# A two-block transformer kernel: block sums of the second chunk placed behind residual additions, and the third layer's deviations computed in a step of their own

## The chip, the core and the metric

One NeuronCore of a Trainium2 chip. The metric is device time in microseconds for one launch, median of several runs; lower is better. The engines are TensorE (PE in the profile, its weight loads PEld), VectorE (DVE), ScalarE (ACT), GpSimd (POOL) and SyncE (SP), which here only issues DMAs. Each works through its own queue of instructions and they meet at semaphores.

## The reference

Four layers in a row on one sequence of 2048 tokens by 1024 features, each added to the residual x:

```python
x = x + _A_ref(_layernorm(x), A_wqkv, A_wo)              # layer 0
x = x + _B_ref(_layernorm(x), B_W_gate, B_W_up, B_W_down)  # layer 1
x = x + _A_ref(_layernorm(x), A_wqkv, A_wo)              # layer 2
x = x + _B_ref(_layernorm(x), B_W_gate, B_W_up, B_W_down)  # layer 3

# _A_ref: linear attention, 32 heads of 32
q, k, v = x @ wqkv;  phi(t) = where(t > 0, t + 1, exp(t)) + 1e-6
o = phi(q) @ (phi(k).T @ v) / (phi(q) . sum(phi(k)) + 1e-6);  result = o @ wo
# _B_ref: gated unit, F = 3584
result = (relu(x @ W_gate) * (x @ W_up)) @ W_down
```

The layer norm subtracts the mean and divides by sqrt(variance + 1e-5), without weights. Inputs and the output are bf16.

## The kernel before

**Tiles.** x stays on chip in fp32 as 16 token tiles of 128 tokens (P = 128, ST = 16). Four tiles make a quarter (QT = 4), two quarters a chunk of 1024 tokens. Layers 1 and 3 (`layer_B`) work on chunk c = 0 and then on c = 1. For each chunk `glu` runs 14 units of gate and up products, and `down` then multiplies the result h by W_down and adds to x.

**Block products.** Most large products are done with seven block products in place of eight (Strassen's scheme in Winograd's form). With four blocks a11, a12, a21, a22 of an operand it needs the sums s1 = a21 + a22, s2 = s1 - a11, s3 = a11 - a21 and s4 = a12 - s2. For the normed and transposed tokens xnT these block sums are made by `sums_x` (L1104, the additions at L1114 to L1117) on VectorE, one call for a pair of token tiles j (one of each quarter of the chunk), four instructions of 128x512 each. `glu` reads them through xs[l, c]; its first product of a later chunk (five, `vg`) reads s1 of all four j.

**The down projection.** `down` runs seven products in the order 11, 21, T1, T2, 22, T3, T4. The large ones (`product`, matmuls at L1253) take 112 or 56 matmuls of 512 columns; each of four PSUM banks is added to x on VectorE when it is done (`onto`, L1266). In layer 3, whose sum is the output, the last addition of a piece goes to a bf16 tile xo (L1273) and is sent to the output. Some products are deep (`deep`, matmuls at L1305): split once more into seven of 14 matmuls of 256 columns. In chunk 0, T1 and 22 are deep in layer 1, and T1, 22 and T4 in layer 3. Within a deep product the order is x = 1, z = 5, y = y + 6, x = x + 2, y = y + 7, z = z + 3, y = y + 4. Before 7 can go onto y, VectorE must have made z from y and m5 (`dz`, L1322; m5 is ScalarE's copy `dm`, L1312). The inner sums of a deep product's operand (h at L1280) are made on VectorE too, shortly before.

**Norms and transposes.** While `down` of chunk 0 runs, the tokens of chunk 1 (quarters 2 and 3) are normed for the same layer by `ln_chunk`. ScalarE makes the normed tile xnb (`ln_norm_sums`, L215 to L221), and `ln_turn` (L400) issues a DMA transpose of it into xnT on SyncE. Eight transposes follow each other, alternating between quarter 2 and quarter 3: the first and second belong to j = 0, the seventh and eighth to j = 3. In layers 0 and 2 `ln_norm` takes statistics on VectorE (L163, L168), and `ln_rstd` takes the reciprocal deviation on ScalarE as exp(-0.5 ln(var + eps)).

**Order.** Work beside the products is put off by `_Later`: `at(delay, fn)` runs fn after so many ticks, and `tick` is called after each product step. `down` of chunk 0 in layer 1 has 54 ticks: 8 for each large product, 7 for each deep one. Ticks 31 and 38 end T2 and 22. So in program order `ln_chunk(l, 1, 20, 3, 3, after)` puts the four calls of `sums_x` at ticks 31, 37, 43 and 49. Outside the `manual_schedule` blocks the framework's planner sets the order of each engine's queue by its own estimate of when operands are ready; an instruction may come out ahead of one written before it. `issue_after(it)` keeps what is written inside it behind the instruction it; `behind` (L265) wraps that.

**Buffers.** Weights, xnT, the sums s and h come from one pool of 16 buffers of 8 KB for each partition (`slot`). A new tile takes a buffer that was released earlier, so the place in the program at which a tile is first asked for decides which buffer it gets and when that is free. Weights come through a ring (`_Ring`) of five tiles ahead, loaded by SyncE.

The names that matter below: `dy`, `dx`, `dz` are the banks of `down` (with T in the name, those of a deep product T1 or T4 in the profile); `w<-td`, `w<-dd`, `w<-ddT` are loads of W_down blocks; `w<-tg`, `w<-tu` loads of the made gate and up blocks; `away<-x` stores of x.

Of the kernel before, what the change touches and what calls it, by code (L numbers as in the profile page):

```python
# [8 lines left out]
ALU = mybir.AluOpType  # L9
ACT = mybir.ActivationFunctionType  # L10
F32 = mybir.dt.float32
# [3 lines left out]
P = 128  # L15
# [2 lines left out]
QT = 4  # L18


LN_AT = ((4, 2), (8, 2), (12, 2), (16, 2), (20, 12), (23, 10), (26, 8), (29, 6))


class _Ring:
# [68 lines left out]
class _Net:  # L93
# [69 lines left out]
        self.nc.vector.bn_stats(out=stats[:, c, :], in_=src[:, c * fmax:(c + 1) * fmax])  # L163

    def ln_rstd(self, stats):
        nc = self.nc
        mv = self.small.tile([P, nc.vector.BN_AGGR_DIM], F32, tag="mv")
        nc.vector.bn_aggr(out=mv, in_=stats)  # L168
        rstd = self.small.tile([P, 1], F32, tag="rstd")
        nc.scalar.activation(out=rstd, in_=mv[:, 1:2], func=ACT.Ln, bias=self.eps5[:, 0:1])  # L170
        self.last_rstd = nc.scalar.activation(out=rstd, in_=rstd, func=ACT.Exp, scale=-0.5)
        return mv, rstd

    def ln_scale(self, src, mv, rstd, xn, h=None):
        w = self.D // 2
# [5 lines left out]
    def ln_norm(self, layer, t):  # L181

        nc = self.nc
        if layer % 2:
            return self.ln_norm_sums(layer, t)
        src = self.xb[t] if layer == 0 else self.x[t]
        stats = self.small.tile([P, 2, nc.vector.BN_STATS_DIM], F32, tag="stats")
        for c in range(2):
            self.ln_stat(t, src, c, stats)
        mv, rstd = self.ln_rstd(stats)  # L190

        def scale():
            if layer % 2 == 0 and (layer, t // QT) != (2, 0):
                return self.ln_scale(src, mv, rstd, self.xn_home(layer, t))
            xn = self.temp([P, self.D], F16, name="xnb") if layer % 2 else self.xn_home(layer, t)
            shift = self.small.tile([P, 1], F32, tag="shift")
            nc.vector.tensor_scalar(out=shift, in0=mv[:, 0:1], scalar1=rstd[:, 0:1], scalar2=-1.0,
                                    op0=ALU.mult, op1=ALU.mult)
            nc.scalar.activation(out=xn, in_=src, func=ACT.Identity, scale=rstd[:, 0:1],
                                 bias=shift[:, 0:1])  # L200
            return xn

        return scale
# [198 lines left out]
    def ln_at(self, delay, layer, t, lag, after=None):  # L402
        def stat():
            with self.tc.issue_after(after) if after else nullcontext():
                scale = self.ln_norm(layer, t)
            self.later.at(1, lambda: norm(scale))

        def norm(scale):
            xn = scale()
            self.later.at(lag, lambda: self.ln_turn(layer, t, xn))  # L410

        self.later.at(delay, stat)

# [40 lines left out]
    def layer_A(self, l, last_ln):  # L454
        nc, G, KT, D = self.nc, self.G, self.KT, self.D
        ring, later = self.ring, self.later
# [32 lines left out]
        def k_unit(q, j, c, between=None):  # L489
            t = q * QT + j  # L490
            pk = self.pk_home(l, t)
            self.phi(project(f"k{c}", q, j, between), pk[:, c * NW:(c + 1) * NW])
            later.at(1 + (10 if self.phi_lag else 0), lambda: k_sum(t, slice(c * NW, (c + 1) * NW)))
# [31 lines left out]
        xn, pk = (lambda i: self.xn[l, i]), (lambda i: self.pk[l, i])  # L525
# [315 lines left out]
        def column_major(f, q):  # L841
            return [lambda j=j, c=c: f(q, j, c) for c in range(H) for j in range(QT)]
# [28 lines left out]
        for i in range(QT if l == 0 else self.NS, self.ST):  # L871
            at, lag = (8 + 3 * (i - QT), 2) if l == 0 else LN_AT[i - self.NS]
            self.ln_at(at, l, i, lag)
            if l:
                later.at(at + 2, lambda i=i: self.send_away(i))
        if l == 0:
            first = self.head_units(lambda *a: k_unit(0, *a), lambda *a: q_unit(0, *a), *steps)
        else:
            first = column_major(k_unit, 0)
# [239 lines left out]
    def ln_chunk(self, l, c, first, step, lag, after):  # L1119
        for j in range(QT):  # L1120
            for h in range(2):
                self.ln_at(first + (2 * j + h) * step, l, (2 * c + h) * QT + j, lag, after)
            self.later.at(first + (2 * j + 1) * step + lag + 5, lambda j=j: self.sums_x(l, c, j))

    def glu(self, l, c, u, hT):

# [81 lines left out]
    def down(self, l, c, hT, final):  # L1208


        nc, later, ring, v = self.nc, self.later, self.ring, self.nc.vector
# [30 lines left out]
        first, second = c * 2 * QT, (c * 2 + 1) * QT  # L1242
# [17 lines left out]
        def onto(ts, cols, src, last):  # L1260

            xs = self.xall[:, ts, cols]
            if len(src.shape) == 2:
                src = src.rearrange("p (t n) -> p t n", n=cols.stop - cols.start)
            if not (final and last):
                v.tensor_tensor(out=xs, in0=xs, in1=src, op=ALU.add)  # L1266
                return
            xo = self.temp([P] + list(xs.shape[1:]), BF16, name="xo")
            m = xs.shape[1]
            split = ts.stop == self.ST and cols.start == 0 and m == 2  # L1270
            for k, queue in zip(range(m) if split else (0,), (nc.scalar if split else nc.gpsimd, nc.sync)):
                s = slice(k, k + 1) if split else slice(0, m)
                v.tensor_tensor(out=xo[:, s, :], in0=xs[:, s, :], in1=src[:, s, :], op=ALU.add)  # L1273
                queue.dma_start(out=self.o_v[:, ts.start + s.start:ts.start + s.stop, cols], in_=xo[:, s, :])

        def sums(ops):
# [150 lines left out]
    def layer_B(self, l, final):  # L1427
        ring = self.ring

        def behind(it, fn):  # L1430
            with self.tc.issue_after(it.ins):
                fn()

        for c in range(2):
            hT = []
            first = l == 1 and c == 0
            wd = {}
            for u in range(self.U):
                if u % 2 == 0:
                    hT.append(self.slot(f"h{l}_{c}_{u // 2}", dtype=F16))  # L1440
                ring.load_to(ring.index((l, c, "g", u)) + 5)
                if first:
                    if u + 1 < self.U:
                        self.later.at(4 if u else 9, lambda u=u: behind(self.last_put if u else self.last_z, lambda: [
                            self.make_gu(ring.get((l, c, w, u + 1)), w, u + 1) for w in "gu"]))
                    if u == 3:
                        for d in (self.U - 4, self.U - 2):
                            wd[d] = self.load_d(d)
                        self.make_dd("22", 18)
                    if u in (4, 5, 6):  # L1450
                        for i, n in enumerate(range(3 * (u - 4), min(3 * (u - 3), 8))):
                            self.later.at(2 + 4 * i, lambda d=self.U - 4 + n // 4 * 2, n=n % 4: behind(
                                self.last_put, lambda: self.sums_d(wd[d], d, (n,))))
                    if u == 7:
                        self.make_dd("T1", 1)
                if not final and c == 1:
                    if u in (0, 3):
                        self.load_w("qk"[u // 3])
                    if u in (1, 2, 4, 5):
                        for n in range(2):  # L1460
                            self.later.at(4 + 5 * n, lambda w="qk"[u // 4], n=2 * (u % 3 - 1) + n: behind(
                                self.last_put, lambda: self.sums_w(w, n)))
                if (l, c, u) in ((1, 1, 6), (3, 0, 4)):
                    self.make_dd("T4" if l == 1 else "21", 1)
                if c == 0 and u == 1:
                    for n, turn in enumerate(self.turns):
                        self.later.at(1 + n, turn)
                if c == 0 and u in (1, 2):
                    self.later.at(6, lambda u=u: behind(self.last_put, self.pairs[u - 1]))
                self.glu(l, c, u, hT)  # L1470
                if c == 0 and u == 2:
                    self.pairs[2]()
                if c == 0 and u == (self.U - 1 if first else 0):
                    after = self.last_put.ins
                if c == 1 and u == 6:
                    held = self.last_put.ins
            if c == 0:
                self.ln_chunk(l, 1, 20, 3, 3, after)
            elif not final:
                self.ln_later(l + 1, 0, 25, 3, 4, held)  # L1480
                self.ln_later(l + 1, 1, 37, 3, 4, held)
            self.down(l, c, hT, final)

    def run(self):
# [56 lines left out]
```

## Time and profile before

| | us |
|---|---|
| median of 3 runs | 1451.38 (1451.16 to 1452.89) |
| the profiled execution, own time | 1451.29 |
| its span | 1449.5 |
| VectorE busy | 959.4 |
| ScalarE busy | 613.8 |
| GpSimd busy | 310.0 |

The profiled execution's own time lies 1.8 us above its span: what runs before the first and after the last recorded instruction. TensorE ran at its full clock in all slices. Down of layer 1, chunk 0 lies at 397 to 479 us of the span, and that of layer 3, chunk 0 at 1117 to 1197 us. In the table of the page's part 2 the DMA engines are busy for four to nine tenths of most slices:

```profile
DMA  9950787997469999646973119978644799444465
```

Each digit is a fortieth of the span (36 us) in tenths. Slices 12 and 13 (counted from 1) hold layer 1's stretch, 32 and 33 that of layer 3.

### The profile page before, as it was taken

How to read it: one execution, taken by the hardware profiler on the slowest of the kernel's cores; microseconds unless marked ns; L12 is line 12 of the kernel's file. 1: busy time of each engine (PE TensorE's matmuls, PEld its weight loads, DVE VectorE, ACT ScalarE, POOL GpSimd, SP SyncE). 2: the span in 40 equal slices, each digit the busy share in tenths (PEclk: the TensorE clock that was granted, in tenths of full speed). 3: DMA queues.
4: the chain of work that ended last, by engine and by line, in shares of the span. 5: the costliest groups of instructions: out<-in, count | busy, mean ns of one | idle time of the engine just before them, and what ended most of it. 6: DMA issues, size and time to landing. Idle time of an engine off the chain costs nothing.

```text
span 1449.5 us, 20266 instructions
## 1 busy us (share of the span) xinstructions
PE 1437.6 (99%) x7430; PEld 709.0 (49%) x7430; DVE 959.4 (66%) x1799; ACT 613.8 (42%) x1113; POOL 310.0 (21%) x221
## 2 busy tenths in 40 slices
PE   9999999999999999999999999999999999999998
PEld 4444444444455444445644444444444564444457
DVE  7978698677594456549688876764445864444595
ACT  7872564233333334332168626633333433333300
POOL 1453861011100011110031586410111011111102
PEclk9999999999999999999999999999999999999999
DMA  9950787997469999646973119978644799444465
GB/s 284 238 161 8 175 215 200 289 331 256 161 217 288 353 312 307 199 128 222 294 244 88 59 32 278 266 230 262 206 145 150 207 279 328 146 145 146 153 236 179
DMA packets 328836, 304.90 MB, mean 210 GB/s; under 512 B 107456, under 2 KB 291776, under 8 KB 327712
## 3 DMA queue, kind: packets, MB, share of 16 engines
q1 hardware_dynamic: 320688, 282.30, 65.5%
q10 hardware_dynamic: 6560, 17.24, 3.2%
q0 software_dynamic: 1488, 4.07, 0.8%
q8 instruction: 58, 0.95, 0.3%
q14 instruction: 42, 0.34, 0.1%
HBM read 227.28 MB, written 51.64 MB: 192 GB/s over the span
## 4 chain that ended last, share of the span: by engine, by line
PE 92%; DVE 4%; ACT 2%; DMA 1%; issue 1%; SPq 0%; ACTq 0%; DVEq 0%
PE yg L1140 10%; PE yu L1140 10%; PE ps L480 10%; PE dy L1253 7%; PE xu L1140 6%; PE xg L1140 6%; PE dx L1253 6%; PE ps L763 4%; PE vg L1140 3%; PE zu L1140 3%; PE vu L1140 3%; PE zg L1140 3%; PE my L562 3%; PE dyT L1305 2%; PE mx L562 2%; PE mv L562 2%
## 5 line engine op out<-in xcount | busy, mean ns | idle before, releaser
L1140 PEld LDWEIGHTS <-w 128*128 128x128 f16 (+1 forms) x3136 | 306.8, 98 | 372.2 <-issue 3.4
L1193 POOL TENSOR_TENSOR h<-m5u,m5g 128x512 f16<-128x512 f32 x56 | 72.6, 1297 | 721.1 <-DVE m5u L1189 648.8
L480 PE MATMUL ps<-w,xnT 128*128 128x512 bf16 x768 | 169.9, 379 | 0.6 <-DMA w<-in_A_wqkv_dram 0.4
L1176 DVE TENSOR_TENSOR zg<-yg,m5g 128x512 f32<-128x512 f32 x56 | 39.1, 698 | 179.5 <-PE yg L1140 175.4
L480 PEld LDWEIGHTS <-xnT 128*128 128x128 bf16 x768 | 74.3, 98 | 90.2 <-issue 1.4
L1140 PE MATMUL yg<-s,w 128*128 128x512 f16 x448 | 115.0, 379 | 0.3 <-DVE zg L1176 0.3
L1140 PE MATMUL yu<-s,w 128*128 128x512 f16 x448 | 114.9, 379 | 0.1
L1140 PE MATMUL xg<-xnT,w 128*128 128x512 f16 x448 | 115.0, 379 | 0.0
L1140 PE MATMUL xu<-xnT,w 128*128 128x512 f16 x448 | 115.0, 379 | 0.0
L1253 PEld LDWEIGHTS <-h 128*128 128x128 f16 x672 | 65.7, 98 | 78.2
L1305 PEld LDWEIGHTS <-h 128*128 128x128 f16 x966 | 94.5, 98 | 15.3 <-issue 3.0
L1148 ACT ACTIVATE m5g<-m5g 128x512 f32<-128x512 f32 x56 | 35.2, 628 | 154.2 <-DVE m5g L1189 154.2
L423 ACT ACTIVATE e<-e,eps 128x512 f32<-128x512 f32 x128 | 91.0, 720 | 3.3
L710 POOL TENSOR_TENSOR kvc<-pq,kvc 128x1024 f32<-128x1024 bf16 x32 | 78.6, 2455 | 53.1 <-DVE den L715 32.7
L1253 PE MATMUL dx<-w,h 128*128 128x512 bf16 x392 | 85.3, 379 | 0.0
L763 PE MATMUL ps<-T,pqT 128*128 128x512 bf16 x384 | 83.6, 379 | 0.0
L1157 ACT ACTIVATE m5g<-vg 128x512 f32<-128x512 f32 x56 | 33.4, 597 | 108.5 <-PE vg L1140 108.5
L1151 DVE TENSOR_TENSOR h<-yu,r 128x512 f16<-128x512 f32 x56 | 38.7, 691 | 52.8 <-PE yu L1140 52.8
L501 POOL TENSOR_TENSOR kvc<-kvc,slab 128x512 f32<-128x512 f32 x46 | 57.3, 1250 | 75.9 <-DVE slab L426 72.7
L1148 ACT ACTIVATE r<-yg 128x512 f32<-128x512 f32 x56 | 33.4, 597 | 85.5 <-PE yg L1140 85.5
L1189 DVE TENSOR_TENSOR m5u<-yu,m5u 128x512 f32<-128x512 f32 x56 | 38.6, 690 | 46.7 <-PE yu L1140 46.7
L422 ACT ACTIVATE e<-ps 128x512 f32<-128x512 f32 x92 | 54.2, 589 | 28.2 <-PE ps L480 27.7
(233 smaller groups left out, 2384.1 us busy)
## 6 DMA issues: line engine op xcount, KB each, us to landing
w<-in_B_W_gate_dram SPq DMA_DIRECT2D x56, 512.0 KB, 6.1
w<-in_B_W_up_dram SPq DMA_DIRECT2D x56, 512.0 KB, 5.9
w<-tg SPq DMA_DIRECT2D x42, 512.0 KB, 7.3
w<-tu SPq DMA_DIRECT2D x42, 512.0 KB, 6.7
w<-ddT SPq DMA_DIRECT2D x21, 896.0 KB, 6.1
w<-td SPq DMA_DIRECT2D x18, 896.0 KB, 4.8
w<-dd SPq DMA_DIRECT2D x15, 896.0 KB, 4.6
w<-in_B_W_down_dram SPq DMA_DIRECT2D x14, 896.0 KB, 4.9
```

Of the source, the lines that this page charges most:

```text
L422: nc.scalar.activation(out=e, in_=ps, func=ACT.Relu, scale=-1.0)
L423: nc.scalar.activation(out=e, in_=e, func=ACT.Exp, scale=-1.0, bias=self.eps6[:, 0:1])
L480: nc.tensor.matmul(by_row(ps), lhsT=self.xnT[l, l_q][:, kt, j * P:(j + 1) * P], rhs=w[:, kt, :].rearrange("p (b i d) -> p i b d", i=R, d=H ...
L501: nc.gpsimd.tensor_tensor(out=ksum[:, cols], in0=ksum[:, cols], in1=pk, op=ALU.add)
L562: nc.tensor.matmul(banks[j], lhsT=A(i)[:, j * P:(j + 1) * P], rhs=B(i), start=start and i == 0, stop=i == NS - 1, skip_group_check=True)
L710: nc.gpsimd.tensor_tensor(out=prod, in0=pq_of[sc, j], in1=zrow, op=ALU.mult)
L763: nc.tensor.matmul(ps, lhsT=pqT[sc][:, g, j * P:(j + 1) * P], rhs=T[g // 4][:, g % 4, n2 * NW:(n2 + 1) * NW], start=(g == 0), stop=(g == G ...
L1140: nc.tensor.matmul(ps, lhsT=W[w][m][:, k, :], rhs=A[m][:, k, :], start=start and k == 0, stop=k == 3, skip_group_check=True)
L1148: self.last_relu = nc.scalar.activation(out=out, in_=ps, func=ACT.Relu)
L1193: nc.gpsimd.tensor_tensor(out=h[:, 3, :], in0=V["u"], in1=V["g"], op=ALU.mult)
L1253: nc.tensor.matmul(banks[j], lhsT=A(k)[:, j * P:(j + 1) * P], rhs=w[:, i, :], start=start and k == 0, stop=k == self.U - 1, skip_group_che ...
L1305: nc.tensor.matmul(bank[:, j * H:(j + 1) * H], lhsT=A[i // 2][:, i % 2, j * P:(j + 1) * P], rhs=B[m][:, i, :], start=start and i == 0 and ...
```

## The change

Two things are changed. `ln_chunk` no longer asks for a call of `sums_x` five ticks after the transpose is issued. It asks for the four calls at ticks 39, 42, 45 and 48, and each is kept behind the last residual addition that `onto` had written by then (`last_on`). And for layer 2 the reciprocal deviation leaves the step that takes the statistics: `ln_norm` stops after `bn_aggr`, the next tick runs `ln_root` (the Ln and Exp pair on ScalarE), and the tick after that scales. The statistics start one tick earlier (LN_AT and the two calls of `ln_later`), and `send_away` keeps its tick.

```diff
--- before.py
+++ after.py
@@ -18,7 +18,7 @@
 QT = 4
 
 
-LN_AT = ((4, 2), (8, 2), (12, 2), (16, 2), (20, 12), (23, 10), (26, 8), (29, 6))
+LN_AT = ((3, 2), (7, 2), (11, 2), (15, 2), (19, 12), (22, 10), (25, 8), (28, 6))
 
 
 class _Ring:
@@ -163,13 +163,16 @@
         self.nc.vector.bn_stats(out=stats[:, c, :], in_=src[:, c * fmax:(c + 1) * fmax])
 
     def ln_rstd(self, stats):
+        mv = self.small.tile([P, self.nc.vector.BN_AGGR_DIM], F32, tag="mv")
+        self.nc.vector.bn_aggr(out=mv, in_=stats)
+        return mv, self.ln_root(mv)
+
+    def ln_root(self, mv):
         nc = self.nc
-        mv = self.small.tile([P, nc.vector.BN_AGGR_DIM], F32, tag="mv")
-        nc.vector.bn_aggr(out=mv, in_=stats)
         rstd = self.small.tile([P, 1], F32, tag="rstd")
         nc.scalar.activation(out=rstd, in_=mv[:, 1:2], func=ACT.Ln, bias=self.eps5[:, 0:1])
         self.last_rstd = nc.scalar.activation(out=rstd, in_=rstd, func=ACT.Exp, scale=-0.5)
-        return mv, rstd
+        return rstd
 
     def ln_scale(self, src, mv, rstd, xn, h=None):
         w = self.D // 2
@@ -187,9 +190,16 @@
         stats = self.small.tile([P, 2, nc.vector.BN_STATS_DIM], F32, tag="stats")
         for c in range(2):
             self.ln_stat(t, src, c, stats)
-        mv, rstd = self.ln_rstd(stats)
-
-        def scale():
+        if layer == 2:
+            mv = self.small.tile([P, nc.vector.BN_AGGR_DIM], F32, tag="mv")
+            nc.vector.bn_aggr(out=mv, in_=stats)
+        else:
+            mv, rstd = self.ln_rstd(stats)
+
+        def scale(rstd=None if layer == 2 else rstd):
+            if rstd is None:
+                rstd = self.ln_root(mv)
+                return lambda: scale(rstd)
             if layer % 2 == 0 and (layer, t // QT) != (2, 0):
                 return self.ln_scale(src, mv, rstd, self.xn_home(layer, t))
             xn = self.temp([P, self.D], F16, name="xnb") if layer % 2 else self.xn_home(layer, t)
@@ -407,7 +417,10 @@
 
         def norm(scale):
             xn = scale()
-            self.later.at(lag, lambda: self.ln_turn(layer, t, xn))
+            if callable(xn):
+                self.later.at(1, lambda: norm(xn))
+            else:
+                self.later.at(lag, lambda: self.ln_turn(layer, t, xn))
 
         self.later.at(delay, stat)
 
@@ -872,7 +885,7 @@
             at, lag = (8 + 3 * (i - QT), 2) if l == 0 else LN_AT[i - self.NS]
             self.ln_at(at, l, i, lag)
             if l:
-                later.at(at + 2, lambda i=i: self.send_away(i))
+                later.at(at + 3, lambda i=i: self.send_away(i))
         if l == 0:
             first = self.head_units(lambda *a: k_unit(0, *a), lambda *a: q_unit(0, *a), *steps)
         else:
@@ -1120,7 +1133,8 @@
         for j in range(QT):
             for h in range(2):
                 self.ln_at(first + (2 * j + h) * step, l, (2 * c + h) * QT + j, lag, after)
-            self.later.at(first + (2 * j + 1) * step + lag + 5, lambda j=j: self.sums_x(l, c, j))
+            self.later.at(39 + 3 * j, lambda j=j: self.behind(
+                self.last_on, lambda j: self.sums_x(l, c, j), (j,)))
 
     def glu(self, l, c, u, hT):
 
@@ -1263,14 +1277,14 @@
             if len(src.shape) == 2:
                 src = src.rearrange("p (t n) -> p t n", n=cols.stop - cols.start)
             if not (final and last):
-                v.tensor_tensor(out=xs, in0=xs, in1=src, op=ALU.add)
+                self.last_on = v.tensor_tensor(out=xs, in0=xs, in1=src, op=ALU.add)
                 return
             xo = self.temp([P] + list(xs.shape[1:]), BF16, name="xo")
             m = xs.shape[1]
             split = ts.stop == self.ST and cols.start == 0 and m == 2
             for k, queue in zip(range(m) if split else (0,), (nc.scalar if split else nc.gpsimd, nc.sync)):
                 s = slice(k, k + 1) if split else slice(0, m)
-                v.tensor_tensor(out=xo[:, s, :], in0=xs[:, s, :], in1=src[:, s, :], op=ALU.add)
+                self.last_on = v.tensor_tensor(out=xo[:, s, :], in0=xs[:, s, :], in1=src[:, s, :], op=ALU.add)
                 queue.dma_start(out=self.o_v[:, ts.start + s.start:ts.start + s.stop, cols], in_=xo[:, s, :])
 
         def sums(ops):
@@ -1477,8 +1491,8 @@
             if c == 0:
                 self.ln_chunk(l, 1, 20, 3, 3, after)
             elif not final:
-                self.ln_later(l + 1, 0, 25, 3, 4, held)
-                self.ln_later(l + 1, 1, 37, 3, 4, held)
+                self.ln_later(l + 1, 0, 24, 3, 4, held)
+                self.ln_later(l + 1, 1, 36, 3, 4, held)
             self.down(l, c, hT, final)
 
     def run(self):
```

## The prediction

> **What bounds the kernel now.** I read the busy shares first, then TensorE's waits, then the place of the longest one engine by engine.
>
> ```profile
> PE 1437.6 (99%) x7430; PEld 709.0 (49%) x7430; DVE 959.4 (66%) x1799; ACT 613.8 (42%) x1113; POOL 310.0 (21%) x221
> ```
>
> TensorE is busy for 1437.6 of 1449.5 us, so a gain can only come from the 12 us in which it stands. Its waits, with total, number and longest:
>
> ```profile
> PE dy L1305 <- DVE dz L1322: 2.8, 1, 2.8
> PE idle L279 <- DVE e L276: 1.4, 1, 1.4
> PE qy L664 <- DVE qz L686: 1.0, 1, 1.0
> ```
>
> The first is one event, the largest of all. In the timeline of TensorE (start, length, operation) it lies in layer 3, chunk 0, in the deep product "22":
>
> ```profile
> 1165.32 1.69 PE L1305 MATMUL dx<-w,h 128*128 128x256 bf16 x14
> 1169.79 1.69 PE L1305 MATMUL dy<-w,h 128*128 128x256 f16 x14 [2.78 <-DVE dz L1322]
> ```
>
> Such groups otherwise start 1.53 us apart (1162.26, 1163.79, 1165.32), so this one was due at 1166.85 and is **2.94 us** late. The 2.78 counts from a modelled end. VectorE at that place:
>
> ```profile
> 1160.03 0.42 DVE L1114 TENSOR_TENSOR s<-xnT 128x512 f16<-128x512 f16 x1
> 1163.61 0.42 DVE L1114 TENSOR_TENSOR s<-xnT 128x512 f16<-128x512 f16 x1 [3.17 <-DMA xnT<-xnb]
> 1164.29 0.68 DVE L1266 TENSOR_TENSOR x<-x,dy 128x512 f32<-128x512 f32 x1
> ...
> 1169.05 0.69 DVE L1322 TENSOR_TENSOR dz<-dy,dm 128x512 f32<-128x512 f32 x1
> ```
>
> The second block sum stood 3.17 us for a DMA transpose; behind it waited a residual addition whose operand was long there, six more sums, the inner sums h and dz, which TensorE needed. The chain of waits goes through the same transpose (1157.96, 5.63 us).
>
> **What the Trainium skill says.** "TensorE: Matmul & The Clock Gate", section "Architectural detail", calls the VectorE queue strict FIFO: one waiting instruction holds all behind it. The trace agrees: the addition at 1164.29 ran only after the sums, although TensorE had finished its bank about 1160.9 (the three before it ran 1.51 us apart, at 1156.40, 1157.91, 1159.42). "Perfetto Trace Analysis", section "Summary: the profiler window per engine type", says that the record of a DMA's issue leaves out the data movement. It does here: this chunk's transposes took 1.2 to 5.5 us to issue and 3.2 to 9.5 us to land. "DMA: Bandwidth & Descriptors", section "Issuing engines are not separate DMA queues", says that all DMAs share 16 engines; so a weight load moved ahead of a transpose can delay it.
>
> **The change part by part.** The built instruction streams of both kernels have the same order on TensorE, ScalarE and GpSimd. Only VectorE and SyncE differ, in two places: layers 1 and 3, second half of the first chunk's down projection.
>
> *Third layer's deviations.* Statistics move a tick earlier, the root pair stays at its old tick, and send_away's delay makes up for LN_AT. No instruction changes its place on any engine in layer 2. Cost 0, bounds -0.2 to +0.2.
>
> *Sums of tiles 0 and 1, layer 3.* The eight (0.34 us apart each, 2.7 us) leave the place before "22" and come after its last addition. Remaining ahead of dz are four h sums, the addition of dm, two h sums. In before that row, from first h (1166.57) to the end of dz (1169.74), takes 3.17 us. When does it start? The first h overwrites an operand of the product dz (at 1162.26), so it waits for TensorE. Layer 1's second chunk has the same row without any block sums:
>
> ```profile
> 699.46 1.10 DVE L1280 TENSOR_TENSOR h<-h,h 128x512 f16<-128x512 f16 x3 [2.04 <-PE dz L1305]
> ...
> 701.95 0.69 DVE L1322 TENSOR_TENSOR dz<-dy,dm 128x512 f32<-128x512 f32 x1
> ```
>
> There product dz began at 698.27, h 1.19 later, dz ended 4.37 after the product's start, and the next dy ran on time at 702.86 (4.59). Carried over: dz ends at 1162.26 + 4.37 = 1166.63, due at 1166.85. Cover 0.22 us; stall left 0, at most 0.3 if h starts only at the product's recorded end. **Gain 2.94** (bounds 2.6 to 2.94).
>
> *The same sums, layer 1, chunk 0.* There they cost VectorE 1.77 us of waiting, but dz ended at 450.07 and TensorE's dy began on time at 450.45. Gain 0.
>
> *Where the sums stand now.* Tiles 0 and 1 run after "22", where VectorE has 4 to 5 us free (it stood 4.50 at 462.79 and 5.39 at 1182.12). Tile 2 now stands before the fourth addition of product T3, tile 3 after it. In layer 1 that addition frees the bank that T4 takes as its fourth: T3 ends at 467.13, three groups of 1.51 later it is 471.66. Behind the third addition (466.4) come three sums (1.0) and the fourth addition (0.7): the sixth transpose must land by about 469.9. In layer 3 the fourth bank is not reused so soon. What counts is T4's dz: due with TensorE's 1192.57 - 2.94 = 1189.63. Working back dz (0.6), dm (0.6), four sums (1.4), the eighth transpose must land by about 1187.0; before it landed by 1185.3.
>
> *SyncE.* The s tiles are taken from the 16 rotating buffers later, so the next five weight tiles get the two buffers earlier and load sooner, and the sixth transpose moves behind loads: in layer 1 behind T3/T4 weights, one gate load, four stores and a tg load; in layer 3 behind two ddT4 loads. In layer 1 it was issued at 453.67. Now the stores wait for additions that end at 455.9 and took 2.7 us to issue, then tg: at the earliest 459.3. Tg took 4.26 us with 0.9 MB of T4 and a gate load just ahead of it; those now go out by about 451, so I take 460. Landing 6.8 us later, as the transpose at 463.57 did: 467, 3 us before it is needed. The eighth should land about 472 to 476 against a need of 478.7 (TensorE's vg at 479.21; before 475.2). In layer 3 the sixth goes at ScalarE's pace, 1167.9, as before; the eighth at about 1175 instead of 1176.4, since ScalarE no longer stands 0.76 us for dz. The DMA share is about 1 over that stretch, so I take its landing as 1184 to 1187. Cost 0, bounds 0 and 1.4.
>
> After layer 3's chunk 0, weight loads wait for buffers that TensorE frees, so they move forward with it: nothing is late next.
>
> Sum: 1451.29 (the profiled execution; span 1449.5 and 1.8 around it) - 2.94 = 1448.35. The median of the runs shown is 1451.38, 0.1 higher: **1448.4**.
>
> **Rivals.**
> 1. *Part is given back in layer 3.* For: transposes issued in a row slow each other (the eighth took 5.46 us to issue behind the seventh) and now three are in a row. If the sixth's 1.9 us are added to 1185.3 the eighth lands at 1187.2, stall 0.2; 3 us more, 1.4. Against: the two ddT4 loads that went just ahead of them are now 6 us or more earlier. Middle 0.8: 1449.2.
> 2. *Nothing is left of it.* Both late landings, layer 1 and layer 3, take about 1.4 each: 1451.2. Against: it needs two independent misses.
> 3. *Slower.* Place: layer 1, sixth transpose, behind four stores that wait for VectorE and behind tg. If SyncE gets to it only at 466.5, when in before it was through with the seventh, and it takes the 9.5 us that the slowest took, it lands at 476.0. The fourth addition then ends at 477.7 and TensorE stands 6.1 us in T4: net +3.2, 1454.6. It decides from a landing of 472.8 on, where the loss passes 2.94. Against: loads worth 1.4 MB are gone from that stretch.
> 4. *More than the forecast.* The transpose's landing varies (3.2 to 9.5), so unprofiled runs may have stood longer: 1447.7.
>
> **How the numbers follow.** Forecast 0.60, rival 1 0.17, rival 2 0.07, rival 3 0.08, rival 4 0.08. The bound of 0.2%, about what a measurement of this kernel can tell from no change, is 2.90 us, almost the gain itself: 1448.48. So the forecast's 0.60 splits, 0.37 faster and 0.23 same: one time in three or so some tenths come back. Faster 0.37 + 0.08 = 0.45; same 0.23 + 0.17 + 0.07 = 0.47; slower 0.08. The forecast's own range is 1448.0 to 1448.9; with rival 1 up to its bound and rival 4 it is 1447.6 to 1450.4, leaving out rivals 2 and 3 and a little of the tails.
>
> **What would show it.** Right: no wait of "dy <- DVE dz" on TensorE; product "22" of layer 3 with starts 1.53 us apart throughout; the first two tiles' sums without a DMA wait; the pieces of layer 2 unchanged in length. Wrong: a wait of T4's dy on VectorE in layer 1 (467 to 472), of vg on s at a chunk's start, or of dyT on dzT in layer 3, with VectorE's sums ended by a transpose just before. A gain under 2.6 us without any of these would mean that dz is held by the h sums or by ScalarE's dm, and that the cover of 0.22 was not there.

## The result and the profile after

The changed kernel takes 1448.17 us (median of 11 runs, 1447.77 to 1449.23) where the kernel before takes 1451.38 (11 runs beside it, 1450.75 to 1454.77). The ratio is 0.9975, with a 95% interval of 0.9966 to 0.9985. The span of the profiled execution went from 1449.5 to 1446.0 us.

Part 1 of the page of the changed kernel (busy time, share, instructions):

```profile
PE 1437.7 (99%) x7430; PEld 709.2 (49%) x7430; DVE 959.7 (66%) x1799; ACT 613.8 (42%) x1113; POOL 309.6 (21%) x221
```

No engine did less work; every busy time is within 0.4 us of before. What shrank is idle time of TensorE. Its waits (what it waited for, total, number, longest):

```profile
PE idle L289 <- DVE e L286: 1.4, 1, 1.4
PE qy L677 <- DVE qz L699: 1.0, 1, 1.0
PE qx L677 <- DVE qy L668: 0.3, 1, 0.3
```

The wait of 2.8 us of dy for dz is gone and these others are as they were. (A wait of 0.7 us at the very head, in the profile of before, is missing too; more on the head below.) The lines of `sums_x` and `down` have moved by 13 or 14: the sums are now L1127 to L1130, the residual addition L1280 and L1287, h L1294, dz L1336, the deep products L1319. TensorE in layer 3's product "22" (start, length, operation):

```profile
1163.20 1.69 PE L1319 MATMUL dy<-w,h 128*128 128x256 f16 x14
1164.73 1.69 PE L1319 MATMUL dx<-w,h 128*128 128x256 bf16 x14
1166.26 1.69 PE L1319 MATMUL dy<-w,h 128*128 128x256 f16 x14
1167.79 1.69 PE L1319 MATMUL dz<-w,h 128*128 128x256 bf16 x14
```

All starts are 1.53 us apart. VectorE at the same place, with idle time and its releaser in brackets:

```profile
1162.86 1.10 DVE L1294 TENSOR_TENSOR h<-h,h 128x512 f16<-128x512 f16 x3 [1.82 <-PE dz L1319]
...
1165.35 0.69 DVE L1336 TENSOR_TENSOR dz<-dy,dm 128x512 f32<-128x512 f32 x1
...
1171.66 0.42 DVE L1127 TENSOR_TENSOR s<-xnT 128x512 f16<-128x512 f16 x1
```

The row from h to dz starts when TensorE's product dz lets it, ends at 1166.04 and so is 0.22 us ahead of 1166.26. The sums come at 1171.66 and wait for no transfer.

Followed event by event, the changed kernel is 0.6 us ahead from its head on, where no instruction has another place: in this execution VectorE stood 2.08 us for the first load of x (before: 2.46) and TensorE 0.20 us for a load of weights (before: 0.41). It is another 2.92 us ahead from layer 3's "22" to the end. So 2.92 of the 3.5 us of span are the change, and the 0.6 are not. That the medians differ by 3.2 us, near 2.92, is in part luck as well: later sets of executions of the kernel before have medians up to 1.7 us longer, as rival 4 at the end shows.

The other place where sums moved is layer 1. VectorE there:

```profile
468.13 0.43 DVE L1127 TENSOR_TENSOR s<-xnT 128x512 f16<-128x512 f16 x1 [2.23 <-DMA xnT<-xnb]
...
469.14 0.68 DVE L1280 TENSOR_TENSOR x<-x,dy 128x512 f32<-128x512 f32 x1
...
474.21 0.43 DVE L1127 TENSOR_TENSOR s<-xnT 128x512 f16<-128x512 f16 x1 [4.05 <-DMA xnT<-xnb]
```

VectorE stood 2.23 us for the sixth transpose and 4.05 for the eighth; TensorE waited for neither. How near both were is the subject of an experiment below.

### The profile page after: what moved, and what is told of

It reads as the page before. It is cut to its first block, busy times and chain, and to the rows that moved or that the text cites. A ratio compares the mean times of both kernels' runs of the same rounds, so it can differ in the third digit from the quotient of the medians.

```text
span 1446.0 us, 20268 instructions
## 1 busy us (share of the span) xinstructions
PE 1437.7 (99%) x7430; PEld 709.2 (49%) x7430; DVE 959.7 (66%) x1799; ACT 613.8 (42%) x1113; POOL 309.6 (21%) x221
## 4 chain that ended last, share of the span: by engine, by line
PE 92%; DVE 5%; ACT 1%; issue 1%; DMA 1%; SPq 0%; DVEq 0%; ACTq 0%
PE yu L1154 10%; PE yg L1154 10%; PE ps L493 10%; PE dy L1267 8%; PE xu L1154 6%; PE xg L1154 6%; PE dx L1267 6%; PE ps L776 4%; PE zu L1154 3%; PE vg L1154 3%; PE vu L1154 3%; PE zg L1154 3%; PE my L575 3%; PE dyT L1319 2%; PE mv L575 2%; PE mx L575 2%
## 5 line engine op out<-in xcount | busy, mean ns | idle before, releaser
L1319 PEld LDWEIGHTS <-h 128*128 128x128 f16 x966 | 94.5, 98 | 12.3
```

Source lines behind the costliest of these rows:

```text
L1319: nc.tensor.matmul(bank[:, j * H:(j + 1) * H], lhsT=A[i // 2][:, i % 2, j * P:(j + 1) * P], rhs=B[m][:, i, :], start=start and i == 0 and ...
```

## Experiments

Theory: TensorE lost 2.94 us in one place, because tile 1's sums stood on VectorE for the fourth transpose ahead of dz. Rivals: the third layer's part did it; the later ticks did it, through SyncE's queue; the wait was not what cost the time. All ratios are to the kernel before, run on the same chip.

### One part alone: third layer's deviations

The third layer is layer 2 in the kernel's counting. (Where an expectation speaks of the third layer's "22" or its first chunk, layer 3 is meant.) All of the change except the edit in `ln_chunk`:

```diff
-            self.later.at(39 + 3 * j, lambda j=j: self.behind(
-                self.last_on, lambda j: self.sums_x(l, c, j), (j,)))
+            self.later.at(first + (2 * j + 1) * step + lag + 5, lambda j=j: self.sums_x(l, c, j))
```

> Only the third layer's part of the change; the block sums stay where they were. Theory (the gain is the removed wait in layer 3's product 22): TensorE still waits 2.8 us for dz there, time as before, 1451.4, within 0.5. Rival (the deviations in their own step carry the gain or a part): 1448.2 to 1450.8, with a shorter wait of qy for qz in layer 2 than the 1.0 us of before.

Measured: 1452.65 against 1453.11 us, ratio 0.9997 (0.9989 to 1.0006). Every engine's queue has the same order as in the kernel before. This part is worth nothing that can be measured. The time itself misses the expected 1451.4 within 0.5, as that of the kernel before beside it does; a likely reason is under rival 4 at the end.

Its profile shows what the wait can do besides. TensorE in "22" of layer 3:

```profile
1165.13 1.69 PE L1318 MATMUL dx<-w,h 128*128 128x256 bf16 x14
1169.97 1.89 PE L1318 MATMUL dy<-w,h 128*128 128x256 f16 x14 [3.15 <-DMA w<-td]
1171.66 3.19 PE L1318 MATMUL dz<-w,h 128*128 128x256 bf16 x14
1174.64 1.73 PE L1318 MATMUL dy<-w,h 128*128 128x256 f16 x14
```

and the stretches around it (bounds, length, busy times of five engines, granted clock of TensorE as a share of its full speed, DMA share, GB/s):

```profile
1170.00:1172.00 2.00, 2.00 (x16) 1.66 (x16) 1.89 (x6) 2.00 (x8) 0.67 (x1) 0.83 1.35 307
1172.00:1174.00 2.00, 2.00 (x11) 1.34 (x10) 1.31 (x4) 2.00 (x3) 0.78 (x2) 0.50 0.77 96
1174.00:1176.00 2.00, 2.00 (x17) 1.66 (x16) 1.78 (x5) 0.43 (x1) 0.13 (x1) 0.82 0.81 206
```

The group is 3.31 us late (due 1165.13 + 1.53 = 1166.66). The releaser named is a weight load, but dz ended at 1169.91, 0.06 before the group began, so it is the same wait. From about 1171.3 on the granted clock is 0.50 for about 3.4 us: the group of 14 matmuls takes 3.19 us instead of 1.69. From 1169.97 to 1176.21, where the next product begins, three groups take 6.24 instead of 3 x 1.53 = 4.59, another 1.65 us lost.

### One part alone: the sums of layer 3, of layer 1

In the kernel before, the new place for one layer only (`l == 3`, and in the other kernel `l == 1`):

```diff
+            if l == 3:
+                self.later.at(39 + 3 * j, lambda j=j: self.behind(
+                    self.last_on, lambda j: self.sums_x(l, c, j), (j,)))
+            else:
+                self.later.at(first + (2 * j + 1) * step + lag + 5, lambda j=j: self.sums_x(l, c, j))
```

> The whole change, but in layer 1 the block sums are asked for at their old ticks; only layer 3's are moved. Theory: the whole gain is in layer 3, 1448.3 (2.9 to 3.3 under before), no wait of dy for dz. Rival (both layers give a part, since VectorE stood for a transpose in both): about half, 1449.8.

> The counterpart: only layer 1's block sums are moved, layer 3's stay. Theory: no gain, 1451.4 within 0.5, and the 2.8 us wait of dy for dz is there in full. Rival (both layers give a part): about 1449.8.

Measured, layer 3 alone: 1448.62 us, ratio 0.9968 (0.9957 to 0.998). Layer 1 alone: 1452.83, ratio 0.9998 (0.999 to 1.0006), with the wait in place:

```profile
PE dy L1309 <- DVE dz L1326: 3.3, 1, 3.3
```

```profile
1163.76 0.43 DVE L1114 TENSOR_TENSOR s<-xnT 128x512 f16<-128x512 f16 x1 [3.73 <-DMA xnT<-xnb]
```

```profile
1164.90 1.69 PE L1309 MATMUL dx<-w,h 128*128 128x256 bf16 x14
1169.94 1.69 PE L1309 MATMUL dy<-w,h 128*128 128x256 f16 x14 [3.34 <-DVE dz L1326]
```

Layer 1's time misses the expected 1451.4 as the one above did, together with the kernel before (1453.11). The whole gain comes from layer 3's sums. The kernel with layer 3 alone showed one thing that the profile of before had not. In layer 1's "22", with the sums at their old place, VectorE stood 2.74 us for the fourth transpose (before: 1.77), and TensorE:

```profile
450.71 1.69 PE L1309 MATMUL dy<-w,h 128*128 128x256 f16 x14 [0.47 <-DVE dz L1326]
```

It is the same pattern as in layer 3 with 0.4 us of slack in the execution of before (dz ended at 450.07, dy began at 450.45). Here it went over by 0.5.

### What counts: the landing

The changed kernel with tiles 0 and 1 back at ticks 31 and 37 and norms and transposes three ticks earlier:

```diff
+            if j < 2:
+                self.later.at(31 + 6 * j, lambda j=j: self.sums_x(l, c, j))
+            else:
...
-                self.ln_chunk(l, 1, 20, 3, 3, after)
+                self.ln_chunk(l, 1, 17, 3, 3, after)
```

> The sums of the first two token tiles go back to their old place ahead of product 22, but the norms and transposes of the second chunk start three ticks earlier. Theory A (what held dz was the landing of the fourth transpose, not the 2.7 us of the sums themselves): if it lands 2.5 us or more earlier against TensorE, no wait of dy for dz is left and the time is 1448.3; for each us less, a us comes back. Theory B (the sums in that row are too long in themselves): a wait of 1 us or more stays even where no sum stands for a transpose, 1449.5 or more.

Measured: 1451.43 us, ratio 0.999 (0.9984 to 0.9997). VectorE and TensorE in layer 3's "22":

```profile
1164.15 0.43 DVE L1127 TENSOR_TENSOR s<-xnT 128x512 f16<-128x512 f16 x1 [2.37 <-DMA xnT<-xnb]
```

```profile
1166.65 1.69 PE L1322 MATMUL dx<-w,h 128*128 128x256 bf16 x14
1170.33 1.69 PE L1322 MATMUL dy<-w,h 128*128 128x256 f16 x14 [1.98 <-DVE dz L1339]
```

The wanted head start hardly came: SyncE still issued this transpose behind the same weight load. Counted from the start of "22" (1162.07 here, 1160.73 before), the sum that waits for it began at 2.08 instead of 2.88, 0.80 earlier. The group is 1170.33 - 1168.18 = 2.15 us late instead of 2.94, 0.79 less. Two profiles above agree: with layer 2's deviations alone the sum began 3.25 us after "22" and the group was 3.31 late, with layer 1's sums alone 3.44 (1163.76 - 1160.32) and 3.51. In all four the stall is 0.06 or 0.07 more than the first number: a microsecond of landing is a microsecond of stall. The median fell by 1.7 us, more than 0.79; the granted clock, under rival 4, is a part of that. Theory B is not settled, since a sum still stood for the transpose in this run; the order alone, next, shows that at least four of the eight sums cost nothing ahead of dz.

### Order or ticks

Two kernels take the two halves of the edit apart: the order kept at the old ticks, and the new ticks without the order.

```diff
-            self.later.at(39 + 3 * j, lambda j=j: self.behind(
+            self.later.at(first + (2 * j + 1) * step + lag + 5, lambda j=j: self.behind(
                 self.last_on, lambda j: self.sums_x(l, c, j), (j,)))
```

> The changed kernel with the block sums at their old ticks (31, 37, 43, 49) but kept behind the last residual addition. What counts is the order on VectorE: tile 1's sums, which wait for the fourth transpose, now stand behind dz of "22" whichever tick is given, and only tile 0's four sums (4 x 0.34 = 1.4 us, their transposes landed before) stand ahead of it, in VectorE's idle time for dz's product. My theory: no wait for dz in layer 3, 1448.2 as the changed kernel has it. Rival (the later ticks do it, since they also move SyncE's issues): the wait of 2.9 us is back, 1451.2 or more.

```diff
-            self.later.at(39 + 3 * j, lambda j=j: self.behind(
-                self.last_on, lambda j: self.sums_x(l, c, j), (j,)))
+            self.later.at(39 + 3 * j, lambda j=j: self.sums_x(l, c, j))
```

> The changed kernel with the block sums at their new ticks (39, 42, 45, 48) but not kept behind the last residual addition; only VectorE's order differs from it. Tick 39 comes after product "22" has issued its seven products, so tile 1's sums, which wait for the fourth transpose, stand behind dz of "22" by the ticks alone. My theory: no wait for dz in the third layer's "22", and about the changed kernel's time, 1448.2 to 1449.2, since the sums now stand ahead of "22"'s last addition, which T3's fourth product waits for. Rival (without the order the wait for the transpose comes ahead of something TensorE needs, only later): a wait of 1 us or more in T3 or T4 of layer 1 or 3, and 1449.5 to 1451.

Measured: order alone 1448.38 us (ratio 0.9968, 0.9956 to 0.998), ticks alone 1448.73 (0.9974, 0.9963 to 0.9984); neither has a wait of dy for dz. With the order alone VectorE in "22":

```profile
1161.59 0.42 DVE L1127 TENSOR_TENSOR s<-xnT 128x512 f16<-128x512 f16 x1
...
1163.49 1.10 DVE L1294 TENSOR_TENSOR h<-h,h 128x512 f16<-128x512 f16 x3 [0.36 <-PE dz L1319]
```

Tile 0's four sums fill the time in which VectorE otherwise stands for TensorE, and SyncE's order is that of the kernel before. So neither SyncE nor the tick is the cause: it is enough that the sums that depend on the fourth transpose are behind dz. The rival that gives the credit to the ticks falls, and so does that of a new wait in T3 or T4. The profile of the ticks alone has a wait of 1.2 us of another kind (xu for ScalarE's yu, at 331 us), in a stretch whose code is untouched; it is in the profile of the earlier transposes too, with 1.0.

### How thin the cover is

Three passes over m5 ahead of dz in that one product:

```diff
             mm(6, S2, y)
+            for _ in range(3 if (l, c, p) == (3, 0, "22") else 0):
+                v.tensor_scalar(out=m5, in0=m5, scalar1=0.0, scalar2=None, op0=ALU.add)
             v.tensor_tensor(out=z, in0=y, in1=m5, op=ALU.add)
```

> The changed kernel with three more passes of VectorE over a 128x512 f32 tile just ahead of dz in product "22" of the third layer's first chunk; the residual addition of dm goes behind dz, and TensorE's order stays. My theory (TensorE has no slack there but the 0.22 us that dz is early, so every us of VectorE beyond it is a us of span): with p the length of one such pass (0.35 to 0.65 us), dz comes 3p - 0.6 later, product 7 of "22" waits 3p - 0.6 - 0.22, that is 0.2 to 1.1 us, and the median goes from 1448.2 to between 1448.4 and 1449.3. Rival (the wait for the transpose was not what cost the time, and VectorE there has room): no wait in "22" and 1448.2.

Measured: 1448.62 us (ratio 0.9973, 0.9963 to 0.9983). VectorE and TensorE:

```profile
1164.90 0.88 DVE L1337 TENSOR_SCALAR dm<-dm 128x512 f32<-128x512 f32 x2
...
1166.70 0.69 DVE L1338 TENSOR_TENSOR dz<-dy,dm 128x512 f32<-128x512 f32 x1
```

```profile
1165.56 1.69 PE L1319 MATMUL dx<-w,h 128*128 128x256 bf16 x14
1167.44 1.69 PE L1319 MATMUL dy<-w,h 128*128 128x256 f16 x14 [0.19 <-DVE dz L1338]
```

One pass takes 0.34 us of the row (the third starts at 1166.03, h behind it at 1166.37), so the expectation's sum is 3 x 0.34 - 0.6 - 0.22 = 0.20. From h to dz the row took 3.01 us (1163.69 to 1166.70) where it took 2.49 in the changed kernel (1162.86 to 1165.35), 0.52 more instead of 0.42. Less the 0.22 of cover that is 0.30, and the group began 1167.44 - 1165.56 - 1.53 = 0.35 us late; the rest is the 0.05 us that pass between the end of dz and the group (1167.39 and 1167.44 here, 1169.74 and 1169.79 in before). (The 0.19 of idle time counts from a modelled end, as 2.78 stood for 2.94 in before.) The median is 0.4 us above the 1448.2 of the changed kernel, which by itself would be within the spread of both; it is the wait in the profile that counts. VectorE has no room there beyond the 0.22; the rival, that it has, falls.

### How near the slower case lay

The four stores of layer 1, chunk 0 issued a second time from GpSimd (the copy writes the same values to the same place):

```diff
+                        later.at(1, lambda i=i: nc.gpsimd.dma_start(
+                            out=self.away[t + 2 * j + i], in_=self.x[t + 2 * j + i]))
```

> The changed kernel with the four stores of layer 1's first chunk issued a second time, from GpSimd's queue, so that the transfers around the sixth transpose of that layer have 1 MB more beside them; the engines' orders stay. It asks how near the slower rival of the prediction lay: the sixth transpose landed at 468.1 and the addition behind its sums ended at 469.8, 1.3 us before product T4 needed it. My theory: up to 1.3 us of delay of that landing costs nothing, beyond it each us costs one; 1 MB at some 260 GB/s is 3.9 us if all of it goes ahead, so the landing comes 0 to 3.9 us later and the run is 0 to 2.6 us longer (1448.2 to 1450.8). Rival (the slack is the 3 us that was forecast): at most 0.9 us longer, and no wait in T4 for a landing below 471.0.

Measured: 1455.52 us (1452.18 to 1457.79), ratio 1.0017 (1.0011 to 1.0024), past what both theories allowed. VectorE and TensorE where the chunk changes:

```profile
468.99 0.42 DVE L1127 TENSOR_TENSOR s<-xnT 128x512 f16<-128x512 f16 x1 [2.78 <-DMA xnT<-xnb]
...
481.09 0.42 DVE L1127 TENSOR_TENSOR s<-xnT 128x512 f16<-128x512 f16 x1 [10.07 <-DMA xnT<-xnb]
...
482.56 2.47 DVE L1280 TENSOR_TENSOR x<-x,dy 128x512 f32<-128x512 f32 x4
```

```profile
459.71 19.37 PE L1267 MATMUL dy<-w,h 128*128 128x512 f16 x89
484.49 1.86 PE L1154 MATMUL vg<-s,w 128*128 128x512 f16 x4 [5.41 <-DVE x L1280]
```

The sixth transpose was hardly later (468.99 against 468.13), and T3 and T4 did not wait. The eighth was: SyncE issued it at 472.43 (468.37 in the changed kernel), behind a weight load (w<-tu) that took 3.72 us to issue instead of 0.57. Its sums began 2.01 us after the modelled end of T4 (479.08), in the changed kernel 4.57 ahead of it (474.21, 478.78), so 6.58 later. Vg began 5.41 us after that end instead of 0.16 ahead of it, so 5.57 late. The slack of the eighth was 6.58 - 5.57 = 1.0 us. The reason is in VectorE's rows: behind the eighth's four sums stand the last residual additions, whose banks vg needs, and vg began 3.4 us after the first sum. The need was 478.62 - 3.40 = 475.2. The same reckoning for the kernel before leaves 0.6 us (479.21 - 3.40 = 475.81, sums at 475.22): it was no safer there. This run asked about the sixth transpose and found the eighth. Windows of the same kernel:

```profile
482.00:484.00 2.00, 0.00 (x0) 0.00 (x0) 1.97 (x5) 0.00 (x0) 0.00 (x0) 0.83 1.06 363
484.00:486.00 2.00, 1.51 (x4) 0.55 (x4) 1.03 (x2) 0.00 (x0) 0.00 (x0) 0.50 1.14 331
...
490.00:492.00 2.00, 2.00 (x10) 0.92 (x9) 0.00 (x0) 1.21 (x3) 0.00 (x0) 0.97 1.03 424
```

Again the clock fell to 0.50, here from inside the wait until about 490. The first four groups from 484.49 took 6.22 us (the fifth began at 490.71), in the changed kernel 3.45 (478.62 to 482.07). The wait cost 5.57 us and the clock 2.77, together 8.3 of the 8.8 by which the span is longer than that of the changed kernel (1454.8, 1446.0).

### A version that goes on from there

TensorE's next wait, 1.0 us of qy for qz in layer 2, has VectorE standing 1.60 us for ScalarE's e, and ScalarE before that 0.63 and 0.27 us for mv, ahead of two of the roots. So the roots were put behind the last exponential:

```diff
-                rstd = self.ln_root(mv)
+                with self.tc.issue_after(self.last_e.ins):
+                    rstd = self.ln_root(mv)
...
-        nc.scalar.activation(out=e, in_=e, func=ACT.Exp, scale=-1.0, bias=self.eps6[:, 0:1])
+        self.last_e = nc.scalar.activation(out=e, in_=e, func=ACT.Exp, scale=-1.0, bias=self.eps6[:, 0:1])
```

> The changed kernel with the reciprocal roots of layer 2's norm put behind the last exponential on ScalarE. In the changed kernel's profile TensorE's only other wait of 1.0 us is qy for qz near 750 us: ScalarE stood 0.63 and 0.27 us for mv ahead of two of the roots, e came late, VectorE stood 1.60 us for e, and qz behind it came late. My theory: with the roots out of the way e comes about 1 us earlier, the wait goes, 1447.2. Rival (the norm behind the roots is then late, and the wait only moves on to what is made of it): no gain or a loss, 1448.2 to 1451.

It took 1447.88 us (ratio 0.9965, 0.9952 to 0.9979). A second time, beside the changed kernel on one chip:

> The changed kernel as it is, on the same chip as the version with the moved roots, so that the two are compared directly: 1448.2, and a granted clock of 1.000, since no wait of TensorE is over 1.5 us.

> The version with the roots of layer 2's norm behind the last exponential, a second time beside the changed kernel. The wait of 1.0 us is gone from its profile, but two waits of 0.3 us came in its place, so 0.4 to 1.0 us are left: 1447.2 to 1447.8 if the changed kernel has 1448.2. If the wait's end only moved the work elsewhere: no difference within 0.3 us.

Measured: changed kernel 1448.25 us (6 runs, 1447.89 to 1449.3; ratio 0.9971, 0.9959 to 0.9983), moved roots 1447.01 (5 runs, 1446.88 to 1448.01; ratio 0.9963, 0.995 to 0.9975). The wait of qy for qz is in neither profile of the new version. That is 1.2 us less on this chip, a little past what was expected, and 28 of the 30 pairs of one run of each favour the moved roots. Over all occasions its 10 runs have a median of 1447.6, the 17 of the changed kernel 1448.2. The intervals of the ratios overlap, so a gain of 0.6 to 1.2 us is likely rather than proven; the wait that went had 1.0. The second profile has a wait of 0.8 us of xu for yu at 331 us, but so, with 1.0 and 1.2, do two profiles above in which the roots stayed: that the moved roots give something back is not shown.

## Why the prediction was right, step by step

- **The bound, and the one wait of 2.94 us: right.** Busy times stayed; TensorE's idle time went. Layer 3's sums alone carry all of it, and over four profiles the stall follows the landing one for one.
- **Third layer's deviations, cost 0: right.** Same queues; ratio 0.9997.
- **Gain 2.94, cover 0.22 us: right.** The shift at "22" is 2.92 and dz is early by 0.22, as the row of layer 1's second chunk had it.
- **Layer 1, gain 0: right for the profiled execution only.** There the old order had 0.4 us of slack, and in one profile 0.47 us of wait. Moved alone, it gave nothing that could be measured.
- **Where the sums stand now: right in direction, mis-sized in slack.** The sixth transpose of layer 1 was guessed to land at 467, 3 us early. It was issued at 458.37 (guess 460), but its sums began at 468.13: 9.8 us, where 6.8 had been taken from another transpose. The addition behind it ended at 469.82; T3 ended at 466.5 and T4 needed it three groups of 1.51 later, at 471.1. The slack was 1.2 us. For the eighth the need was put at 478.7, when vg starts; the residual additions behind its sums were left out. It was 475.2, and the landing at 474.2 left 1.0. The forecast had that landing at 472 to 476 in the time of before, where the need was 475.8: a short wait lay within its own range, and that none came was luck.
- **SyncE, cost 0: right.** With SyncE's order of before, the time is the same (1448.38).
- **Rivals 1 and 2** did not happen: T4 and vg of layer 1 did not wait, in layer 3 the sums of tile 3 began at 1185.36 without a wait, and dzT ran at 1187.72 after 0.20 us of waiting for its own product, not for a sum.
- **Rival 3** is a real mechanism at another transpose. For the eighth a wait begins at a landing of 475.2, 1 us behind the measured one, and outweighs the gain from 475.2 + 2.9 = 478.1 on, without what the clock adds.
- **Rival 4** (executions may stand longer) has something to it, by a route that the prediction did not name. Of 84 executions of the kernel before in the three later sets, 74 show a granted clock of 0.997 to 0.999. In the largest set (42) the 39 of these have a median of 1453.20, and the three at 1.000 take 1450.6 to 1451.5; in the second (29) the three at 1.000 take 1451.9 to 1453.1 against a median of 1452.98, in the third (13) four take 1449.9 to 1451.2 against 1453.14. Of the changed kernel's 17 executions, 16 show 1.000.

  One stretch of 3.4 us at half clock is 1.7 us, and 1.7 / 1450 = 0.0012 of the mean clock. So it is likely, though only one execution with both was profiled, that the three later sets put the kernel before at 1452.8 to 1453.1 because of the wait of some 3 us and, in most executions, 1.7 us or more of half clock after it.

  The forecast of 1448.4 holds for all sets, since the changed kernel has neither. The gain of 2.94 does not: beside the later sets it is 4.5 to 4.6 us (layer 3 alone, order alone, and the changed kernel itself). The time at half clock, which the prediction put at nothing, seems to have been little in the set of the result (its median of 1451.38 lies near those at full clock; only its profile's clock, 1.000, is on record), and that the gain came out near 2.94 there is luck. Where both kernels ran on one chip (the third set), the four executions of before at full clock have a median of 1450.91 and the changed kernel 1448.25, 2.7 us apart.

## What to carry to other kernels

An instruction that waits for a transfer belongs behind everything on its engine that TensorE needs sooner, even if the transfer is usually in time; here moving it cost nothing and the order alone was enough. When work is moved, its slack is counted to the last instruction queued behind it that TensorE waits for, not to its own consumer. In this kernel a wait of TensorE of about 3 us cost its length and, in most executions by the clock on record, at least 1.7 us of lost clock on top.

## What the runs showed of the hardware

The Trainium skill, "TensorE: Matmul & The Clock Gate", section "What's actually happening", describes a free-running window of 3413 ns, after an idle one of which the clock falls to half. The traces agree on the length: 3.4 us at 0.50 after a gap of 3.31 us, and about 6.8, two such stretches, around one of 5.57 (each counted as the lateness of the group behind it). They do not bear out that a whole window must be idle. The gap of 3.31 us is shorter than 3413 ns, and TensorE was at work again from 1169.97 while the clock fell about 1171.3 (0.83 over 1170 to 1172 is 0.68 us at half). Nor does the length of the gap alone decide: one of 3.51 us in the profile with layer 1's sums alone and one of 2.94 in the profile of before left the clock at 1.00. A window that runs freely would explain that the same gap counts in one execution and not in the next, but where the windows began is not in these profiles. The section "Why this matters for your kernels" of the same page says to keep gaps under about 3 us. The kernel whose profile shows a gap of 2.15 us had a clock under 1.000 in 9 of 20 executions. The eight sets whose profiles show no wait of TensorE above 1.4 us (the changed kernel twice, layer 3 alone, order alone, ticks alone, the padded dz, the moved roots twice) had it in 2 of 53, at 0.999 and without a longer time. How long the gap was in the nine was not seen, so whether 2 us are enough stays open.
